# A distance-only bias in a fused attention and MLP kernel: forward and backward rows, put in place through a skewed DRAM scratch, in a new order

## The chip, the cores and the metric

The kernel runs on one core of one Trainium2 chip. A core has five engines that run side by side and meet at semaphores: PE (TensorE, matrix products), DVE (VectorE), ACT (ScalarE), POOL (GpSimd) and SP (SyncE, which here issues every DMA). The metric is device microseconds (us) of one execution, as the median of several. The profile is of one more execution of the same program.

## The reference

Three stages follow each other. `q`, `k` and `v` have the shape (2 batches, 8 heads, 576 positions, 64).

```python
scores = scale * np.matmul(q, k.transpose(0, 1, 3, 2))
psi_rel = np.log1p(np.abs(pos[:, None] - pos[None, :]))
psi_i = np.log1p(np.maximum(pos[:, None], 1.0))
x = (psi_rel / psi_i)[..., None]
h = np.maximum(x @ w1 + b1, 0.0)          # 32 hidden units
bias = h @ w2                             # one value per head
scores = scores + bias.transpose(2, 0, 1)[None]
attn = softmax(scores); out = attn @ v
# then, on 1152 tokens of 512 values:
h = x @ w_in; x = (h * clip(h + 3, 0, 6) / 6) @ w_out         # 512 -> 2048 -> 512
h = x @ w_in2; x = (rational function of h) @ w_out2          # 512 -> 2048 -> 512
```

The part that the change touches is `bias`: for each pair (i, j) of positions a 32-unit layer of one input, summed to 8 heads. For a fixed row i it depends on j through |i - j| alone. It is the same for both batches.

## The kernel before, in words

The first third of the kernel is attention, the rest the two MLPs. Attention goes by five chunks of query rows (`qc`): four of 128 rows and one of 64, which is taken for both batches at once. For a chunk and a pair of heads, `scores` puts q times k into PSUM (L473; L488 in the last chunk), `logits` on DVE adds the bias tile to it and takes the row maximum (L496), ACT takes the exponential (L662), PE transposes the result in pieces of three 128-column blocks (L680), ACT or DVE copies the pieces out (L688, L690), and `av` multiplies by v (L508). A table, `EV_ENG`, says which engine copies which piece, `OUT_ENG` the same for the copies behind `av` (L712, L714).

The bias of a chunk is a tile `biases[qc]` of 128 rows x (8 heads x 576 columns), from a pool of two buffers (`huge`). It is made by groups `G` of 16 rows, 36 groups in all. The 128 partitions hold 4 rows x 32 hidden units, so a group takes four *units* (`bias_unit`): `relu(psi + threshold)` over 576 columns, on DVE (L431) or ACT (L429) by the table `U_ENG`. `psi` is the table log1p(|distance|) of 1152 columns per partition, of which a unit reads a window of 576 that is shifted by the row; the last four groups use a second table. `bias_sums` (L438) sums the hidden units to heads: for each half of 288 columns four matmuls with 32 output partitions each into one PSUM bank, so two banks a group. `bias_scaled` scales each half into a row buffer `wk` on ACT (L447) or DVE (L449) by the table `SC_ENG`, and `bias_out` (L458) issues one DMA that puts the 16 x 8 rows of 576 values into `biases[qc]`, directly in SBUF. The rows of a group stand 8 apart in the chunk. `unit_logits` needs all groups of its chunk.

Units come in pairs in tiles of the pool `big` (11 buffers), row buffers from `wk` (5 buffers), PSUM banks of sums, transposes and `av` from one pool of 4 (`h`), and a pair's scores take the whole of the pool `ps2`.

Each of these steps is put in a list with `at(time, function, ...)`. The order in which the program is written, and so the order of instructions in each engine's queue, is a table of numbers, `ORDER`, over that list. Each engine works strictly through its own queue.

Of the kernel before, what the change touches and what calls it, by code (L numbers as in the profile page):

```python
# [31 lines left out]
W2 = 2 * S  # L32
PS0 = S - P
# [4 lines left out]
U_ENG = (1, 1, 0, 0, 0, 0, 0, 0, 1, 1, 0, 0, 0, 0, 0, 0, 1, 0, 0, 0, 0, 0, 1, 0, 0, 0, 1, 1, 0, 0, 1, 1, 0, 0, 0, 0, 0,  # L38
# [3 lines left out]
EV_ENG = (1, 1, 1, 1, 1, 1, 1, 0, 1, 1, 1, 0, 1, 0, 1, 1, 1, 0, 0, 0, 1, 1, 1, 1, 1, 1, 1, 0, 0, 1, 1, 1, 0, 0, 1, 0, 1,  # L42
# [3 lines left out]
OUT_ENG = (1, 1, 0, 0, 1, 1, 1, 0, 0, 1, 0, 0, 0, 0, 0, 1, 1, 0, 1, 0)  # L46
X_DVE = (0, 0, 0, 0, 0, 0, 0, 0, 0)
SC_ENG = (1, 1, 1, 1, 1, 1, 0, 0, 1, 0, 1, 1, 1, 1, 1, 1, 1, 1, 1, 1, 1, 1, 1, 1, 1, 1, 1, 1, 0, 1, 1, 1, 0, 0, 0, 0, 1,
    1, 1, 0, 1, 0, 0, 1, 0, 0, 1, 0, 1, 0, 0, 0, 0, 0, 0, 1, 0, 0, 0, 1, 0, 0, 0, 0, 0, 0, 0, 0, 0, 0, 0, 0)
PTX = (1,) * 20 + (0,) * 20  # L50
N_EARLY = 5
ORDER = (0, 26, 1, 2, 24, 25, 27, 16, 28, 29, 3, 4, 30, 34, 32, 22, 42, 35, 33, 43, 50, 48, 36, 40, 51, 49, 41, 320, 37,
# [177 lines left out]
def fused_kernel(ctx: ExitStack, tc, q, k, v, moe_w_in, moe_w_out, moe2_w_in, moe2_w_out,  # L230
# [116 lines left out]
    with tc.manual_schedule():  # L347
# [776 lines left out]
```

## Time and profile before

| | |
|---|---|
| median of 3 runs | 592.98 us (591.97 to 593.93) |
| profiled execution | 594.1 us, of which the span from the first to the last instruction is 592.3 us |
| attention | to about 190 us of the span |
| the two MLPs | from there to the end |
| PE busy over the span | 98% |
| DVE, ACT, POOL busy | 79%, 66%, 33% |

Times in the rows are microseconds from the start of the span. A matmul in fp32 is recorded as two, so `x32` of L438 is 16 matmuls, two groups. A busy share of PE counts the modelled end of a matmul, so the chain of work that ended last is the better witness of what bounds the end. The column PEclk is the granted clock of TensorE as a share of full speed.

### The profile page before, as it was taken

The page shows a single profiled execution, that of the slowest core. Times are in us where ns is not written, and L with a number is a line of the kernel's source. Part 1 is how long each engine was busy: PE and PEld are TensorE (multiplying, and loading weights), DVE is VectorE, ACT ScalarE, POOL GpSimd, SP SyncE. Part 2 cuts the span into 40 slices and gives each one's busy share as a digit, 9 for nine tenths or more (in the row PEclk, how much of TensorE's full clock was granted, in tenths as well). Part 3 has the DMA queues.
Part 4 walks back from the last instruction along what each step waited for, and adds up shares of the span by engine and source line. Part 5 has one row for each costly group of instructions (what it writes and reads, how often), then busy time and mean ns, then how long its engine had stood idle before and what let it go on. Part 6 is the DMA issues. An engine that isn't in the chain of part 4 may idle for free.

```text
span 592.3 us, 11318 instructions
## 1 busy us (share of the span) xinstructions
PE 578.5 (98%) x4291; PEld 509.7 (86%) x4291; DVE 467.8 (79%) x952; ACT 390.1 (66%) x806; POOL 197.1 (33%) x186
## 2 busy tenths in 40 slices
PE   5999999999999999999999999999999999999996
PEld 4458776777788999999999999998898989989985
DVE  7688987788786867685647489888899989999773
ACT  4897886787766636343232344688889878888861
POOL 1000010011005624232003220655576756766632
PEclk8899999999999999999999999999999999999999
DMA  7697423113515352443313122510111313200112
GB/s 220 141 296 168 116 65 87 54 42 99 166 59 178 107 176 77 143 145 140 107 35 91 53 79 100 178 41 32 45 64 39 97 44 107 72 0 1 37 54 71
DMA packets 32119, 56.63 MB, mean 96 GB/s; under 512 B 2488, under 2 KB 19128, under 8 KB 32064
## 3 DMA queue, kind: packets, MB, share of 16 engines
q1 hardware_dynamic: 32064, 55.91, 31.9%
q8 instruction: 33, 0.54, 0.4%
q14 instruction: 22, 0.18, 0.1%
HBM read 41.75 MB, written 2.36 MB: 74 GB/s over the span
## 4 chain that ended last, share of the span: by engine, by line
PE 94%; ACT 2%; DMA 2%; issue 1%; DVE 1%; SPq 0%; ACTq 0%; DVEq 0%
PE h L337 34%; PE y L1005 33%; PE h L508 7%; PE ps L473 7%; PE h L680 6%; PE h L438 5%; DMA kraw<-in_k_dram 2%; PE h L755 1%; ACT wk L447 1%; PE ps L488 1%; ACT big L429 1%; SPq L526 0%; DVE part L1035 0%; ACT big L662 0%; PE h L729 0%
## 5 line engine op out<-in xcount | busy, mean ns | idle before, releaser
L337 PE MATMUL h<-xt,huge 128*128 128x384 f32 x504 | 93.5, 335 | 0.0
L337 PEld LDWEIGHTS h<-xt,huge 128*128 128x128 f32 x504 | 88.2, 188 | 1.1
L855 POOL TENSOR_TENSOR huge<-wk,huge 128x512 fp32r<-128x512 f32 x28 | 36.1, 1296 | 94.8 <-ACT huge L846 69.1
L782 POOL TENSOR_TENSOR xt<-oT,xt 128x512 fp32r<-128x512 f32 x9 | 11.5, 1288 | 168.3 <-ACT xt L776 168.3
L496 DVE CUSTOM_DVE_ANT_0 big<-ps,huge 128x576 f32<-128x576 f32 (+1 forms) x72 | 52.6, 760 | 18.2 <-PE ps L473 16.1
L337 PE MATMUL h<-xt,big 128*128 128x384 f32 x360 | 66.6, 335 | 0.0
L899 ACT ACTIVATE e<-h,cons 128x384 f32<-128x384 f32 x43 | 25.0, 582 | 61.4 <-PE h L337 61.1
L951 POOL TENSOR_TENSOR e<-e,e 128x384 f32<-128x384 f32 x48 | 49.0, 1022 | 44.6 <-ACT e L939 38.8
L337 PEld LDWEIGHTS h<-xt,big 128*128 128x128 f32 x360 | 63.0, 188 | 0.5
L662 ACT ACTIVATE big<-big,mx 128x576 f32<-128x576 f32 (+1 forms) x72 | 56.1, 785 | 6.4 <-DVE mx L496 6.1
L924 POOL TENSOR_TENSOR gl<-e,gh 128x384 fp32r<-128x384 f32 x48 | 49.1, 1028 | 26.4 <-ACT gh L916 15.2
L337 PE MATMUL h<-xt,wp 128*128 128x384 f32 x288 | 53.9, 335 | 0.0
L337 PEld LDWEIGHTS h<-xt,wp 128*128 128x128 f32 x288 | 50.7, 188 | 1.1
L473 PE MATMUL ps<-kraw,rawq 64*128 64x288 f32 x256 | 41.4, 438 | 6.6 <-DMA kraw<-in_k_dram 5.7
L680 PEld LDWEIGHTS h<-csm,big 128*128 128x128 f32 x328 | 35.4, 142 | 8.9 <-issue 4.8
L438 PE MATMUL h<-big,wblk 128*32 128x288 f32 x576 | 41.8, 419 | 0.9 <-ACT wk L447 0.5
L431 DVE TENSOR_SCALAR big<-psw,thr 128x576 f32<-128x576 f32 x94 | 42.5, 511 | 0.0
L680 PE MATMUL h<-csm,big 128*128 128x128 f32 x328 | 41.5, 277 | 0.3 <-ACT xt L688 0.3
L916 ACT ACTIVATE gh<-h 128x384 fp32r<-128x384 f32 x43 | 21.1, 491 | 28.6 <-PE y L1005 19.8
L905 DVE SCALAR_TENSOR_TENSOR h<-e,h 128x384 f32<-128x384 f32 x43 | 24.0, 558 | 20.1 <-ACT e L899 20.0
L473 PEld LDWEIGHTS ps<-kraw,rawq 64*128 64x128 f32 x256 | 22.9, 190 | 19.1 <-issue 10.7
L855 POOL TENSOR_TENSOR big<-wk,big 128x512 fp32r<-128x512 f32 x21 | 27.1, 1296 | 35.8 <-ACT big L846 22.7
(125 smaller groups left out, 1330.4 us busy)
## 6 DMA issues: line engine op xcount, KB each, us to landing
big<-in_moe_w_in_dram SPq DMA_DIRECT2D x32, 512.0 KB, 3.7
big<-in_moe_w_out_dram SPq DMA_DIRECT2D x32, 512.0 KB, 3.5
huge<-wk SPq DMA_DIRECT2D x40, 288.0 KB, 4.2
kraw<-in_k_dram SPq DMA_DIRECT2D x4, 576.0 KB, 8.9
rawq<-in_q_dram SPq DMA_DIRECT2D x4, 512.0 KB, 7.6
vraw<-in_v_dram SPq DMA_DIRECT2D x8, 256.0 KB, 6.2
out_dram<-part SPq DMA_DIRECT2D x5, 256.0 KB, 2.0
out_dram<-psw SPq DMA_DIRECT2D x3, 256.0 KB, 2.7
```

The lines of the kernel that those rows point to most:

```text
L337: nc.tensor.matmul(ps, wx[:, c, :], xx[:, c, :], start=(i == c == 0), stop=(i == 2 and c == KC - 1))
L431: eng.tensor_scalar(dst, win, thr[:, g:g + 1], 0.0, op0=ALU.add, op1=ALU.max)
L438: nc.tensor.matmul(ps[32 * ct:32 * ct + 32, :HS], wblk.rearrange("p i h -> p (i h)"), units_of[G, ct][:, hf * HS:(hf + 1) * HS], start=Tru ...
L473: nc.tensor.matmul(ps[e][:, 512 - HS * (1 - c):512 + HS * c] if c else ps[e][:, 512 - HS:512], x[r, b, hp, :], kraw[r, hp, S * b + HS * c: ...
L496: nc.vector.tensor_tensor_reduce(ss, ps, biases[qc][:, h * S:h * S + n], op0=ALU.add, op1=ALU.min, scale=-0.125, scalar=3e38, accum_out=mx)
L508: nc.tensor.matmul(o[64 * e:64 * e + 64], vraw[:, m, 2 * hp + e, :], pt[e][:, coff + c, cols], start=(c == 0), stop=(c == 4), tile_positio ...
L662: nc.scalar.activation(ss, ss, AF.Exp, bias=mxs[u // 2][:, b, u % 2:u % 2 + 1], scale=-1.0, accum_out=sums[qc][:, b, h:h + 1])
L680: nc.tensor.transpose(ps[:, c - c0], pes[u][:, c * P:(c + 1) * P], ident)
L855: nc.gpsimd.tensor_tensor(lo, held.pop(("wt", it)).bitcast(F32), hi.bitcast(F32), op=ALU.subtract)
L924: eng.tensor_tensor(gl, src, gh.bitcast(F32), op=ALU.subtract)
L951: nc.gpsimd.tensor_tensor(vq, vq, ab, op=ALU.mult)
L1005: nc.tensor.matmul(ys[c][d][:, :TC if L == 0 else DM], lhs, rhs, start=(first and i == 0), stop=(last and i == 2))
```

## The change

A group is now 16 consecutive rows. Its units are computed for the distances 0, 1, ..., n - 1 alone, where n is the larger of `16 G + 16` and `576 - 16 G`: 576 for the first group, 304 in the middle, 576 for the last, and 15,840 columns over the 36 groups, where there were 20,736. All units read the same window of one table of 576 columns, and the second table with its load and its sign step is gone. `bias_sums` takes a whole bank of up to 512 columns at once and a second, short one where n is over 512: 44 banks, where there were 72. `bias_scaled` writes the sums into a row buffer of 591 values: forwards for j >= i, and backwards (a source with step -1) for j < i, in two pieces, or three where there are two banks: 80 pieces in all, where there were 72. `bias_out` now stores these rows into a scratch tile in DRAM with a row step of one element more than the pitch, which shifts each of the 16 rows by its own place. When all groups of a chunk are stored, `load_bias` loads the chunk's bias tile back, two heads to a DMA (four DMAs a chunk, eight for the last). `unit_logits` needs the load of its own two heads.

All tables are new. By them DVE makes 126 of the 144 units (ACT 18; before, 101 and 43), ACT makes 56 of the 80 scaled pieces (16,003 of their 21,276 columns; before, 37 of 72), ACT copies out 101 of the 112 transposed pieces (before 75) and all 20 results of `av` (before 9).

```diff
-W2 = 2 * S
-PS0 = S - P
+DPI = S + 32
+PSA = 512
...
-OUT_ENG = (1, 1, 0, 0, 1, 1, 1, 0, 0, 1, 0, 0, 0, 0, 0, 1, 1, 0, 1, 0)
+OUT_ENG = (1, 1, 1, 1, 1, 1, 1, 1, 1, 1, 1, 1, 1, 1, 1, 1, 1, 1, 1, 1)
...
-ORDER = (0, 26, 1, 2, 24, 25, 27, 16, 28, 29, 3, 4, 30, 34, 32, 22, 42, 35, 33, 43, 50, 48, 36, 40, 51, 49, 41, 320, 37,
+ORDER = (0, 25, 1, 21, 23, 2, 26, 16, 3, 22, 24, 27, 28, 5, 29, 4, 76, 30, 66, 32, 31, 77, 33, 41, 84, 34, 57, 42, 85,
...
-def row_base(G, ct):
-
-    qc, g = divmod(G, 8)
-    return P * qc + g + (32 if qc < 4 else 16) * ct
+def group_rows(G):
+
+    return 16 * G, 16 * G + 16
+
+
+def distances(G):
+
+    r0, r1 = group_rows(G)
+    return max(r1, S - r0)
+
+
+def bank_spans(G):
+
+    n = distances(G)
+    return [(0, n)] if n <= 512 else [(0, 512), (512, n)]
+
+
+def row_pieces(G):
+
+    r0, r1 = group_rows(G)
+    r = []
+    for i, (a, b) in enumerate(bank_spans(G)):
+        if min(b, S - r0) > a:
+            r.append((i, a, min(b, S - r0), False))
+        if min(b, r1) > max(a, 1):
+            r.append((i, max(a, 1), min(b, r1), True))
+    return r
...
+    psi = np.broadcast_to(np.log1p(np.arange(S, dtype=np.float32))[None, :], (P, S))
...
+    rows = np.arange(S).reshape(NG, 16)
...
         def bias_unit(G, ct, eng):
 
-            g, r = 4 * G + ct, row_base(G, ct)
+            g, n = 4 * G + ct, distances(G)
             if ct % 2 == 0:
-                two = BIG([P, 2, S], F32)
+                two = BIG([P, 2, n], F32)
                 units_of[G, ct], units_of[G, ct + 1] = two[:, 0], two[:, 1]
-            dst = units_of[G, ct]
-            win = psiw[:, S - r:2 * S - r] if G < 32 else psit[0][:, S - r:2 * S - r]
+            dst, win = units_of[G, ct], psiw[:, :n]
...
         def bias_sums(G):
 
-            for hf in range(2):
+            outs[G] = []
+            for a, b in bank_spans(G):
                 ps = BANK()
                 for ct in range(4):
-                    nc.tensor.matmul(ps[32 * ct:32 * ct + 32, :HS], wblk.rearrange("p i h -> p (i h)"),
-                                     units_of[G, ct][:, hf * HS:(hf + 1) * HS],
-                                     start=True, stop=True, tile_position=(0, 32 * ct))
-                outs[G, hf] = ps
-
-        def bias_scaled(G, hf, eng):
-            if hf == 0:
-                rows_of[G] = W([P, 2, HS], F32)
+                    nc.tensor.matmul(ps[32 * ct:32 * ct + 32, :b - a], wblk.rearrange("p i h -> p (i h)"),
+                                     units_of[G, ct][:, a:b], start=True, stop=True, tile_position=(0, 32 * ct))
+                outs[G].append((a, ps))
+
+        def bias_scaled(G, k, eng):
+
+            r0, r1 = group_rows(G)
+            i, a, b, back = row_pieces(G)[k]
+            if k == 0:
+                rows_of[G] = W([P, S + 15], F32)
+            a0, ps = outs[G][i]
+            src = ps[:, a - a0:b - a0]
+            if back:
+                src = bass.AP(tensor=src.tensor, offset=src.offset + b - a - 1, ap=[list(src.ap[0]), [-1, b - a]])
+                dst = rows_of[G][:, r1 - b:r1 - a]
+            else:
+                dst = rows_of[G][:, r1 - 1 + a:r1 - 1 + b]
             if eng is nc.scalar:
-                nc.scalar.activation(rows_of[G][:, hf], outs.pop((G, hf))[:, :HS], AF.Copy, scale=rps[:, G:G + 1])
+                nc.scalar.activation(dst, src, AF.Copy, scale=rps[:, G:G + 1])
             else:
-                nc.vector.tensor_scalar(rows_of[G][:, hf], outs.pop((G, hf))[:, :HS], rps[:, G:G + 1], None, op0=ALU.mult)
+                nc.vector.tensor_scalar(dst, src, rps[:, G:G + 1], None, op0=ALU.mult)
 
         def bias_out(G):
 
             qc, g = divmod(G, 8)
-            flat = rows_of.pop(G).rearrange("p a j -> p (a j)")
-            if qc not in biases:
+            if qc not in stored:
+                stored[qc] = T(dpool, [P if qc < 4 else 64, NH * DPI], F32, f"rows{qc}")
+            t = stored[qc]
+            dst = bass.AP(tensor=t.tensor, offset=t.offset + 16 * g * NH * DPI, ap=[[NH * DPI + 1, 16], [DPI, NH], [1, S + 15]])
+            nc.sync.dma_start(dst, rows_of.pop(G))
+
+        def bias_in(qc, hp):
+
+            if hp == 0:
                 new_bias(qc)
-            if qc < 4:
-                nc.sync.dma_start(biases[qc][g::8, :NH * S], flat)
-            else:
-                for rep in range(2):
-                    nc.sync.dma_start(biases[qc][64 * rep + g:64 * rep + 64:4, 64 * rep:64 * rep + NH * S], flat)
+            t, n = stored[qc], P if qc < 4 else 64
+            src = bass.AP(tensor=t.tensor, offset=t.offset + 15 + 2 * hp * DPI, ap=[[NH * DPI, n], [DPI, 2], [1, S]])
+            for rep in range(1 if qc < 4 else 2):
+                nc.sync.dma_start(biases[qc][n * rep:n * rep + n, 64 * rep + 2 * hp * S:64 * rep + 2 * (hp + 1) * S], src)
...
-        at(-9.9, load, "psiw1", psiw[:, PS0:], cpsi[:, PS0:W2])
-        at(-9.85, load, "psiw0", psiw[:, :PS0], cpsi[:, :PS0])
+        at(-9.9, load, "psiw0", psiw[:, :PSA], cpsi[:, :PSA])
+        at(-9.85, load, "psiw1", psiw[:, PSA:], cpsi[:, PSA:])
...
-        at(POS[4] - 14, load_psit)
...
+        def load_bias(qc, hp):
+            need(*(("out", G) for G in range(8 * qc, min(8 * qc + 8, NG))), *((("rows", qc, 0),) if hp else ()))
+            bias_in(qc, hp)
+            done.add(("rows", qc, hp))
...
-            for hf in range(2):
-                at(t + .65 + .05 * hf, group_scaled, G, hf, (nc.vector, nc.scalar)[SC_ENG[2 * G + hf]])
+            for i in range(len(row_pieces(G))):
+                at(t + .65 + .05 * i, group_scaled, G, i, (nc.vector, nc.scalar)[SC_ENG[3 * G + i]])
             at(t + .8, group_out, G)
+        for qc in range(5):
+            for hp in range(NPAIR):
+                at(POS[qc] - .1 + .02 * hp, load_bias, qc, hp)
...
             need(("scores", qc, h // 2, b))
-            need(*(("out", G) for G in range(8 * qc, min(8 * qc + 8, NG))))
+            need(("rows", qc, h // 2))
```

PE, the start of the program: `h` is a PSUM bank, `big` a pair of units, `ps` scores. Before:

```order
L566 MATMUL h_91<-ones_79 128x128 x13
L438 MATMUL h_137<-big_124,wblk_89 32x288 x2
L438 MATMUL h_137<-big_122,wblk_89 32x288 x2
L438 MATMUL h_142<-big_124,wblk_89 32x288 x2
L438 MATMUL h_142<-big_122,wblk_89 32x288 x2
L473 MATMUL ps_26_152<-kraw_83,rawq_114 128x288
```

The same place in the change:

```order
L600 MATMUL h_93<-ones_81 128x128 x13
L462 MATMUL h_143<-big_130,wblk_91 32x512 x2
L462 MATMUL h_143<-big_134,wblk_91 32x512 x2
L462 MATMUL h_148<-big_130,wblk_91 32x64 x2
L462 MATMUL h_148<-big_134,wblk_91 32x64 x2
L512 MATMUL ps_28_159<-kraw_85,rawq_117 128x288
```

One group stands ahead of the first scores in both. Behind these, 13 groups stand ahead of the second scores before, and 15 in the change; the first `av` has 17 groups ahead of it before, and 21 in the change.

SP, the DMA queue, from the last stores of chunk 0's bias on. Before, `huge` is the bias tile itself and the first row is the last but two of chunk 0:

```order
L458 DMA huge_178<-wk_273 16x8x576
L458 DMA huge_178<-wk_279 16x8x576
L458 DMA huge_178<-wk_311 16x8x576
L458 DMA huge_339<-wk_316 16x8x576
L387 DMA vraw_84<-in_v_dram 128x512
```

In the change, `rows_33` and `rows_69` are the scratch of chunks 0 and 1, and `huge_336` the bias tile of chunk 0:

```order
L491 DMA rows_33_175<-wk_275 16x8x591
L491 DMA rows_33_175<-wk_294 16x8x591
L412 DMA vraw_86<-in_v_dram 128x512
L491 DMA rows_69_318<-wk_302 16x8x591
L500 DMA huge_336<-rows_33_175 128x2x576
L491 DMA rows_69_318<-wk_321 16x8x591
L491 DMA rows_69_318<-wk_346 16x8x591
L491 DMA rows_69_318<-wk_352 16x8x591
L491 DMA rows_69_318<-wk_365 16x8x591
L500 DMA huge_336<-rows_33_175 128x2x576 x2
```

The first load of the bias tile waits for all stores of its chunk. The second and third stand behind four stores of the next chunk; the fourth follows only behind the other eight loads of v and the last load of k.

## Rows read from the trace of the kernel before

**Rows 1.** Page, busy time: engine, us, share of the span, instructions.
```profile
PE 578.5 (98%) x4291; PEld 509.7 (86%) x4291; DVE 467.8 (79%) x952; ACT 390.1 (66%) x806; POOL 197.1 (33%) x186
```
**Rows 2.** Page, the chain that ended last, by engine and by line.
```profile
PE 94%; ACT 2%; DMA 2%; issue 1%; DVE 1%; SPq 0%; ACTq 0%; DVEq 0%
PE h L337 34%; PE y L1005 33%; PE h L508 7%; PE ps L473 7%; PE h L680 6%; PE h L438 5%; DMA kraw<-in_k_dram 2%; PE h L755 1%; ACT wk L447 1%; PE ps L488 1%; ACT big L429 1%; SPq L526 0%; DVE part L1035 0%; ACT big L662 0%; PE h L729 0%
```
**Rows 3.** Windows, all engines: stretch, length, busy (instructions), clock, DMA share, GB/s.
```profile
core 0: us, PE busy (x) PEld busy (x) DVE busy (x) ACT busy (x) POOL busy (x), PEclk, DMA share, GB/s
0.00:33.00 33.00, 24.60 (x258) 13.31 (x258) 23.15 (x57) 20.64 (x39) 1.62 (x10) 0.90 0.71 189
33.00:48.07 15.07, 14.66 (x125) 8.81 (x125) 12.63 (x34) 13.76 (x36) 0.00 (x0) 1.00 1.06 292
48.07:70.00 21.93, 21.93 (x292) 17.26 (x294) 19.25 (x50) 17.95 (x42) 0.00 (x0) 1.00 0.54 137
70.00:105.00 35.00, 35.00 (x406) 24.75 (x399) 28.19 (x70) 27.26 (x63) 2.60 (x2) 1.00 0.33 83
105.00:140.00 35.00, 35.00 (x407) 26.74 (x406) 28.03 (x72) 27.80 (x65) 2.80 (x4) 1.00 0.21 55
140.00:175.00 35.00, 35.00 (x433) 26.86 (x428) 26.81 (x67) 25.41 (x62) 2.52 (x2) 1.00 0.38 108
```
**Rows 4.** Windows of L438 alone: PE and PEld busy (records), clock, DMA.
```profile
0.00:33.00 33.00, 17.55 (x224) 7.42 (x224) 0.90 0.71 189
33.00:48.07 15.07, 3.53 (x48) 1.25 (x48) 1.00 1.06 292
```
**Rows 5.** The chain in order of time: start, us, what.
```profile
3.55 10.04 DMA kraw<-in_k_dram
...
48.14 4.52 PE h L508 x80
...
59.45 2.08 PE h L438 x32
```
**Rows 6.** Timeline of DVE to 34 us: start, us, what, idle before it.
```profile
5.46 8.24 DVE L431 TENSOR_SCALAR big<-psw,thr 128x576 f32<-128x576 f32 x19
19.78 0.52 DVE L449 TENSOR_SCALAR wk<-h,csm 128x288 f32<-128x288 f32 x1 [6.09 <-PE h L438]
...
21.92 9.96 DVE L431 TENSOR_SCALAR big<-psw,thr 128x576 f32<-128x576 f32 x23
32.34 0.76 DVE L496 CUSTOM_DVE_ANT_0 big<-ps,huge 128x576 f32<-128x576 f32 x1 [0.46 <-PE h L438]
```
**Rows 7.** Groups by shape to 190 us: count, busy, mean ns, idle before.
```profile
L429 ACT ACTIVATE big<-psw,thr 128x576 f32<-128x576 f32 x34 | 25.1, 777 | 3.2 <-DVE psw L601 3.2
...
L688 ACT ACTIVATE xt<-h 128x384 f32<-128x384 f32 x42 | 18.1, 496 | 11.1 <-PE h L680 11.1
...
L447 ACT ACTIVATE wk<-h,csm 128x288 f32<-128x288 f32 x37 | 17.1, 514 | 3.7 <-PE h L438 2.8 <-DMA huge<-wk 0.9
...
L712 ACT ACTIVATE oT<-h 128x256 f32<-128x256 f32 x7 | 2.7, 385 | 1.6 <-PE h L508 1.5
...
L601 DVE TENSOR_SCALAR psw<-psw,tb 128x704 f32<-128x704 f32 x1 | 0.6, 577 | 0.0
...
L601 DVE TENSOR_SCALAR psw<-psw,tb 128x448 f32<-128x448 f32 x1 | 0.4, 443 | 0.0
```
**Rows 8.** DMA from 24 to 50 us: packets and issues, KB each, us to landing.
```profile
DMA packets 3246, 6.88 MB, mean 265 GB/s; under 512 B 376, under 2 KB 376, under 8 KB 3242
...
huge<-wk SPq DMA_DIRECT2D x11, 288.0 KB, 8.0
vraw<-in_v_dram SPq DMA_DIRECT2D x8, 256.0 KB, 6.2
```
**Rows 9.** Page, DMA issues of the whole run, us to landing.
```profile
big<-in_moe_w_in_dram SPq DMA_DIRECT2D x32, 512.0 KB, 3.7
...
huge<-wk SPq DMA_DIRECT2D x40, 288.0 KB, 4.2
...
out_dram<-part SPq DMA_DIRECT2D x5, 256.0 KB, 2.0
```

More of the change, by code (lines that the diff above doesn't have):

```diff
@@ L183 @@
 S_PSQ, S_RPS, S_MSK, S_ID, S_W, S_END = 0, 144, 180, 212, 340, 350
-def row_base(G, ct):
-    qc, g = divmod(G, 8)
-    return P * qc + g + (32 if qc < 4 else 16) * ct
+def group_rows(G):
[15 more added lines that the diff above has]
+    return r
 def _constants():
     p = np.arange(P)
-    u = np.arange(W2)[None, :]
-    psi = np.log1p(np.abs(np.concatenate([u - S - 8 * (p // HID)[:, None], u[:, :640] - S - 4 * (p // HID)[:, None]],
-                                         axis=1)).astype(np.float32))
+    psi = np.broadcast_to(np.log1p(np.arange(S, dtype=np.float32))[None, :], (P, S))
     psi_i = np.log1p(np.maximum(np.arange(S, dtype=np.float32), np.float32(1.0)))
-    rows = np.array([[row_base(G, ct) + (8 if G < 32 else 4) * il for ct in range(4) for il in range(4)] for G in range(NG)])
+    rows = np.arange(S).reshape(NG, 16)
     psq = psi_i[rows.reshape(144, 4)[:, p // HID].T]
@@ L203, in _constants @@
     sel = (np.arange(4 * P)[None, :] // HD == np.arange(NH)[:, None]).astype(np.float32)
-    return {"csel": sel, "cpsi": psi.astype(np.float32), "csmall": np.ascontiguousarray(small)}
+    return {"csel": sel, "cpsi": np.ascontiguousarray(psi), "csmall": np.ascontiguousarray(small)}
 def _rows(ap, parts, n):
@@ L349, in fused_kernel @@
         scores_ctx = ctx.enter_context(ExitStack())
+        dpool = ctx.enter_context(tc.tile_pool(name="dpool", bufs=1, space=DRAM))
         apool = actx.enter_context(tc.tile_pool(name="apool", bufs=1))
@@ L353, in fused_kernel @@
         csm = T(apool, [P, S_END], F32, "csm")
-        psiw = T(cpool, [P, W2], F32, "psw")
+        psiw = T(cpool, [P, S], F32, "psw")
         sel = T(apool, [NH, 4 * P], F32R, "sel")
@@ L395, in fused_kernel @@
         wblk = T(apool, [P, 4, NH], F32, "wblk")
-        psit = {}
         def bias_constants():
@@ L408, in bias_weights @@
                                     w2b.unsqueeze(1).to_broadcast([P, 4, NH]), op=ALU.mult)
-        biases, units_of, outs, rows_of = {}, {}, {}, {}
+        biases, units_of, outs, rows_of, stored = {}, {}, {}, {}, {}
         def new_bias(qc):
@@ L527, in load @@
             done.add(key)
-        def load_psit():
-            psit[0] = BIG([P, 640], F32)
-            load("psit", psit[0], cpsi[:, W2:])
         def load_x(fn, nm, m):
@@ L571, in group_unit @@
         def group_unit(G, ct, eng):
-            need(*((("psiw sign", 0),) + ((("psiw sign", 1),) if row_base(G, ct) > S - PS0 else ()) if G < 32 else ("psit sign",)))
+            need(("psiw sign", 0), *((("psiw sign", 1),) if distances(G) > PSA else ()))
             if ct % 2:
@@ L581, in group_sums, with group_scaled @@
             done.add(("sums", G))
-        def group_scaled(G, hf, eng):
-            need(("sums", G), *((("bias", G, 0),) if hf else ()))
-            bias_scaled(G, hf, eng)
-            done.add(("bias", G, hf))
+        def group_scaled(G, k, eng):
+            need(("sums", G), *((("bias", G, 0),) if k else ()))
+            bias_scaled(G, k, eng)
+            done.add(("bias", G, k))
         def group_out(G):
-            need(("bias", G, 0), ("bias", G, 1), *((("out", G // 8 * 8),) if G % 8 else ()))
+            need(*(("bias", G, k) for k in range(len(row_pieces(G)))), *((("out", G // 8 * 8),) if G % 8 else ()))
             bias_out(G)
+            del outs[G]
             done.add(("out", G))
+        def load_bias(qc, hp):
+            need(*(("out", G) for G in range(8 * qc, min(8 * qc + 8, NG))), *((("rows", qc, 0),) if hp else ()))
+            bias_in(qc, hp)
+            done.add(("rows", qc, hp))
         def bias_start():
@@ L598, in psiw_sign @@
         def psiw_sign(late):
-            need("thr", f"psiw{1 - late}")
-            part = psiw[:, :PS0] if late else psiw[:, PS0:]
+            need("thr", f"psiw{late}")
+            part = psiw[:, PSA:] if late else psiw[:, :PSA]
             nc.vector.tensor_scalar(part, part, sgn, None, op0=ALU.mult)
             done.add(("psiw sign", late))
-        def psit_sign():
-            need("thr", "psit")
-            nc.vector.tensor_scalar(psit[0], psit[0], sgn, None, op0=ALU.mult)
-            done.add("psit sign")
         def weights():
```

10 lines of the change are left out of this document (5 added, 5 removed), and 260 rows, old and new, of tables (EV_ENG, ORDER, U_ENG).

## The prediction, made before the changed kernel had run

> **What bounds the kernel now.** I read the page's busy shares first, then the chain that ended last, then windows over attention. The shares give PE 98% of the span [rows 1]; since a busy PE is not a PE at its peak, the chain is what settles it: 94% of it is PE, and the matmuls of the bias (L438) are 5% of the chain, some 30 us, although they compute nothing that ends up in an MLP [rows 2]. The windows show two parts of attention. To 48.07 us, where the first product with v begins [rows 5], PE is not the bound: it has 24.6 of 33 us at a granted clock of 0.90 [rows 3], it stands in its queue for the first k until 13.6 us [rows 5], DVE loses 6.09 us behind a copy that waits for PE, and the first logits come at 32.34 us [rows 6]. The DMA engines are full from then on: share 1.06 at 292 GB/s from 33 to 48 us [rows 3]. From 48.07 us PE is busy without a gap, 35.00 of every 35 us at clock 1.00, with DVE at 77 to 88% and ACT at 73 to 82% [rows 3]. So what is taken off PE behind 48 us comes off the end, if the others keep up; what is taken off ahead of it counts only as far as the first product with v comes earlier.
>
> **PE behind the first product with v.** Ahead of it L438 has 224 + 48 = 272 records [rows 4], 17 groups at 16 records, so 19 groups stand behind it. Two groups take 2.08 us there [rows 5], one 1.04 us: 19 x 1.04 = 19.8 us. In the change 21 groups stand ahead and 15 behind, with 352 to 576 distances each: 6,960 columns (352, 368, ... 576). By columns, 1.04 us / 576 = 1.8 ns each, they take 12.6 us. The gain is 7.2 us. No row shows a bank of 512 columns, nor the short second bank of 16 to 64 columns that four of these groups need. Its bounds: the short bank costs what its columns cost, 160 columns or 0.3 us in all four, or as much as a bank of 288, 0.52 us each, 2.1 us; then the gain is 5.4 us. At the other end, a tenth of a bank's price that does not depend on its columns would make 19 banks in place of 38 cheaper by another 0.3 us. I take 7.2, for the price follows columns wherever the banks are long, and these are nearly all.
>
> [...]
>
> **The opening, up to the first product with v.** Before the first logits, DVE had 44 units and 3 scaled halves: at 9.96 / 23 = 0.43 us a unit in a run [rows 6] these are 19 + 1.6 us from 5.46 us on, 26 us, and with the 6.09 us of idling 32.2, which is where the logits came. In the change 58 units of 455 columns on average stand ahead of the first logits. A unit gets shorter by 0.52 ns a column (577 less 443 ns for 256 columns [rows 7]), so it takes 0.43 - 121 x 0.00052 = 0.37 us, and all of them 21.4 us: 27 us without a stall. No scaled piece stands in DVE's queue there, so the 6.09 us as such go. What is late next is a buffer: the units have 11 buffers of two, and PE gives none back between the first group and the arrival of k, since the first scores stand in the same place of its queue. DVE fills its 11 by about 12 us (5.5 + 16 x 0.41) and goes on when the second group is summed at about 17 us: 5 us lost, 32 us for the first logits. The bounds are 27 and 33.
>
> Beside it runs the detour through DRAM. The units of chunk 0 are complete after 30 of DVE's units, about 23 us with that stall; one group's sums and scaling behind it make 25 us. Then the last store and the first load follow each other, where one transfer was: 4.2 us for a store if it goes as the bias rows did, 2.0 if it goes as the stores of the output, and 3.7 us for a load of similar size [rows 9]. That is 30.7 to 33 us, near the 32 of DVE. The load stands on SP behind the stores it waits for, and behind it stand four stores of chunk 1 and the second and third load; ACT, which has only 5 row buffers, waits for those stores.
>
> [...]
>
> What the transfers do to each other is the larger unknown. Up to the last chunk of v, SP's queue holds from the second group on 13 stores of 0.30 MB, 3 loads of 0.59 MB and 2.4 MB of v: 8.1 MB. Before, 10 stores, v, one q and one k made 6.4 MB. The 1.7 MB more take 6 us at the mean of 265 GB/s of this stretch [rows 8]; at worst, all of chunk 0's loads, 2.36 MB, come on top at that rate: 8.9 us. But before, the engines had room until about 24 us, and a store to DRAM, 2.0 us against 4.2 [rows 9], promises a better rate than the transfers inside SBUF that it replaces. So the first product with v comes between 44 us (the DVE bound, then the same 15.7 us from logits to product as before) and 57 us. I take 49.6, or 1.5 us later than before.
>
> **ACT.** By durations of [rows 7]: 43 units become 18 shorter ones, 33.4 less 11.7 = -21.7 us; scaling goes from 37 x 0.514 to 56 pieces, 28.7, or +9.7; 26 more copies of transposes at 0.496 (five of them narrower) +12.4; 11 more of the results +4.0. Together +4.4 us. DVE is relieved: the units cost no more (126 shorter against 101), while 11 scaled pieces, 26 transposed pieces and 11 results leave it. In PE's dense part ACT goes from 98.4 of 126.9 us, 78% [rows 3], to some 83%, and the wait that could come in place of the removed work is a PE transpose that finds no free bank because a copy waits in ACT's queue behind an exponential. Before, DVE took every third copy. Its bounds are 0 and the whole 4.4 us; I take 1.0, since at 80% PE had no gap.
>
> What has no price: the smaller psi table and the second table that goes come off a load and one DVE step that nothing waited for. The MLPs are unchanged, and their weights are loaded and split by DVE, ACT and POOL, which finish attention earlier too.
>
> **The sum**, against the profiled execution: 594.1 - 7.2 + 1.5 + 1.0 = 589.4 us. That execution is 1.1 us above the median shown, 592.98, so the same sum for a median is 588.3 us.
>
> **Rivals.** *The opening gets shorter.* If the buffers come back sooner, the first logits are nearer to 27 us and the product with v comes at 44: 594.1 - 7.2 - 4 + 1 - 1.1 = 582.8. For it: the stall behind the copy [rows 6] is gone. Against it: k comes no earlier, and the DMA queue is longer.
>
> *ACT becomes the bound of the dense part.* All 4.4 us stand on the path: 594.1 - 7.2 + 1.5 + 4.4 - 1.1 = 591.7. For it: ACT now has nine of ten copies that free PE's banks. Against it: 83% on average.
>
> *The detour through DRAM costs more than PE saves.* Its place is the stretch from 24 to 50 us, where the engines are full [rows 3, 8], and v stands behind three loads in one queue. With 2.36 MB at 265 GB/s, 8.9 us, it is 594.1 - 7.2 + 8.9 + 1 - 1.1 = 595.7. It decides from the point at which the first product with v begins later than 56 us. For it: every bias byte now moves twice, and each row of the scratch starts at another odd place, which no row here has. Against it: the mean of 265 GB/s is held down by the transfers inside SBUF, 8.0 us to landing against 6.2 for v [rows 8].
>
> **How the numbers follow.** This kernel's runs differ so that about 0.3%, 1.8 us, can be told from no change: 591.2 to 594.8 is no change. My forecast, 584 to 591 by its own bounds, has 0.52; the shorter opening 0.18; ACT as the bound 0.14; the costly detour 0.16. So faster 0.70, no change 0.14, slower 0.16. The range from 582 to 594.5 leaves out the costly detour and little below.
>
> **What the profile after would show.** L462 with about 32 us of busy time in place of 41.8, and groups behind the first product with v at 1.8 ns a column, say 0.92 us at 512; the first logits at 31 to 33 us; the first product with v at 48 to 52; PE without gaps from there, the waits on ACT's copies about 1 us in all. The forecast is wrong if PE waits for v or for a bias load for over 4 us, if waits of transposes or sums on ACT come to several us, if long banks cost more than their columns, or if the MLPs begin to wait for weights.

## The result, and the profile after

The changed kernel takes 584.59 us (median of four runs, 584.04 to 585.33) against 592.48 (591.85 to 593.93) for the kernel before on the same chip: a ratio of 0.9864 [0.984, 0.9889], 7.9 us less. The profiled execution took 585.12 us, with a span of 583.2 where it was 592.3.

The page of after, busy time, and the chain that ended last by engine, as [rows 1, 2]:

```profile
PE 572.6 (98%) x4067; PEld 503.5 (86%) x4067; DVE 450.7 (77%) x928; ACT 389.8 (67%) x837; POOL 198.2 (34%) x186
...
PE 93%; DMA 3%; DVE 2%; ACT 1%; SPq 0%; issue 0%; POOL 0%; DVEq 0%; ACTq 0%; POOLq 0%
```

PE still bounds the kernel, with 5.9 us less to do. Where the 9.1 us of span went shows when the span is cut at the first product with v (48.14 us before, 46.02 after) and at the end of attention. Windows of after, columns as in [rows 3]:

```profile
0.00:46.02 46.02, 40.92 (x312) 20.84 (x314) 38.05 (x110) 34.14 (x81) 1.61 (x10) 0.96 0.87 283
46.02:180.50 134.48, 134.48 (x1608) 104.17 (x1609) 92.49 (x237) 109.78 (x278) 12.54 (x12) 1.00 0.53 165
180.50:583.20 402.70, 397.25 (x2150) 378.50 (x2149) 320.13 (x582) 245.85 (x479) 184.01 (x165) 1.00 0.25 79
```

The opening is 2.1 us shorter; what follows the first product with v is 7.0 us shorter (592.3 - 48.14 = 544.2 before, 583.2 - 46.02 = 537.2). In the second window PE is busy in all of its 134.48 us, with ACT at 82%. Windows of L462, the sums of the bias, behind the first product with v: busy time (records):

```profile
46.02:190.00 143.98, 12.96 (x152) 3.95 (x152) 1.00 0.50 155
```

The same window of L438 before is

```profile
48.07:190.00 141.93, 20.72 (x304) 8.75 (x304) 1.00 0.35 96
```

so 7.8 us less there. How the opening runs now is read from the chain in order of time (start, us, what). It begins with `bcoef`, a load of 1 KB: a step of ACT that reads it (`babs`) stands ahead of the first scaled rows in ACT's queue.

```profile
3.88 5.99 DMA bcoef<-in_moe_b_dram
9.89 0.02 ACT babs L1092
...
12.90 6.42 PE h L462 x55
...
19.54 3.75 DMA rows<-wk
...
23.34 5.03 DMA huge<-rows
...
28.54 0.76 DVE big L535
...
30.33 1.23 PE ps L512 x6
...
46.02 4.52 PE h L547 x80
```

and from the timelines of DVE and of PE (start, us, what, idle before it):

```profile
5.32 21.33 DVE L454 TENSOR_SCALAR big<-psw,thr 128x496 f32<-128x496 f32 x58
28.54 0.76 DVE L535 CUSTOM_DVE_ANT_0 big<-ps,huge 128x576 f32<-128x576 f32 x1 [1.90 <-DMA huge<-rows]
```

```profile
9.00 1.24 PE L512 MATMUL ps<-kraw,rawq 64*128 64x288 f32 x8 [0.28 <-DMA kraw<-in_k_dram]
29.36 0.75 PE L512 MATMUL ps<-kraw,rawq 64*128 64x288 f32 x2 [1.61 <-DVE mx L535]
```

Three things differ from [rows 5, 6]. The first scores come at 9.00 us; before, PE waited for k, and they ran from 13.72 us, in a stretch with a granted clock of 0.50 (14 to 18 us), into which PE came after standing idle for k for 5.68 us. DVE makes its 58 units in one go, in 21.33 us, nearly the 21.4 that the prediction had worked out, without the 5 us of idle time that it put on top. And the first logits, at 28.54 us, wait for the detour: last store 3.75 us, first load 5.03 us, of which DVE waits out 1.90.

Why k is earlier is in the DMA rows to 16 us: KB each, us from issue to landing. Before, then after:

```profile
kraw<-in_k_dram SPq DMA_DIRECT2D x3, 576.0 KB, 10.0
rawq<-in_q_dram SPq DMA_DIRECT2D x1, 512.0 KB, 7.7
psw<-in_cpsi_dram SPq DMA_DIRECT2D x1, 352.0 KB, 3.2
...
psw<-in_cpsi_dram SPq DMA_DIRECT2D x1, 224.0 KB, 3.3
...
bcoef<-in_moe_b_dram SPq DMA_DIRECT2D x1, 1.0 KB, 7.0
```

```profile
kraw<-in_k_dram SPq DMA_DIRECT2D x3, 576.0 KB, 6.9
...
rawq<-in_q_dram SPq DMA_DIRECT2D x1, 512.0 KB, 4.5
psw<-in_cpsi_dram SPq DMA_DIRECT2D x1, 256.0 KB, 2.8
...
psw<-in_cpsi_dram SPq DMA_DIRECT2D x1, 32.0 KB, 2.7
...
bcoef<-in_moe_b_dram SPq DMA_DIRECT2D x1, 1.0 KB, 6.0
```

`bcoef` is a constant of the second MLP, 128 partitions of 8 bytes each. By the old order it was issued ahead of q and k, by the new one behind the first of both. It takes 7.0 and 6.0 us here, and 4.3 and 7.4 in the two runs below that move it. A second thing differs ahead of q and k: the psi table (`psw`), 576 KB in two loads before and 288 KB in the change.

### The profile page after: what moved, and what is told of

Its sections match the earlier page's. It is cut to its first block, busy times and chain, and to the rows that moved or that the text cites. A ratio compares the mean times of both kernels' runs of the same rounds, so it can differ in the third digit from the quotient of the medians.

```text
span 583.2 us, 10935 instructions
## 1 busy us (share of the span) xinstructions
PE 572.6 (98%) x4067; PEld 503.5 (86%) x4067; DVE 450.7 (77%) x928; ACT 389.8 (67%) x837; POOL 198.2 (34%) x186
## 4 chain that ended last, share of the span: by engine, by line
PE 93%; DMA 3%; DVE 2%; ACT 1%; SPq 0%; issue 0%; POOL 0%; DVEq 0%; ACTq 0%; POOLq 0%
PE h L361 34%; PE y L1042 32%; PE h L547 7%; PE h L717 7%; PE ps L512 6%; PE h L462 4%; DMA bcoef<-in_moe_b_dram 1%; PE h L792 1%; DMA huge<-rows 1%; DMA big<-in_moe_w_out_dram 1%; PE ps L527 1%; DMA rows<-wk 1%; DVE part L1072 0%; ACT wk L480 0%; DVE h L305 0%
## 5 line engine op out<-in xcount | busy, mean ns | idle before, releaser
L361 PE MATMUL h<-xt,huge 128*128 128x384 f32 x504 | 93.1, 335 | 0.9 <-DVE wk L307 0.9
L361 PEld LDWEIGHTS h<-xt,huge 128*128 128x128 f32 x504 | 88.0, 188 | 2.0 <-DVE wk L307 1.2
L361 PE MATMUL h<-xt,big 128*128 128x384 f32 x360 | 66.1, 334 | 0.0
L361 PEld LDWEIGHTS h<-xt,big 128*128 128x128 f32 x360 | 62.9, 188 | 0.5
L988 POOL TENSOR_TENSOR e<-e,e 128x384 f32<-128x384 f32 x48 | 49.0, 1020 | 37.8 <-ACT e L976 34.8
L361 PE MATMUL h<-xt,wp 128*128 128x384 f32 x288 | 52.8, 335 | 0.0
L361 PEld LDWEIGHTS h<-xt,wp 128*128 128x128 f32 x288 | 50.5, 188 | 0.6
L454 DVE TENSOR_SCALAR big<-psw,thr 128x336 f32<-128x336 f32 (+17 forms) x126 | 49.1, 456 | 0.0
L717 PEld LDWEIGHTS h<-csm,big 128*128 128x128 f32 x328 | 35.6, 142 | 8.1 <-issue 4.6
L717 PE MATMUL h<-csm,big 128*128 128x128 f32 x328 | 41.7, 279 | 0.0
L462 PE MATMUL h<-big,wblk 128*32 128x512 f32 (+17 forms) x352 | 35.8, 485 | 1.9 <-DVE big L454 1.2
L982 ACT ACTIVATE e<-h,acoef 128x384 f32<-128x384 f32 x48 | 32.0, 667 | 7.7 <-PE h L361 7.0
L1014 DVE SCALAR_TENSOR_TENSOR e<-e,acoef,h 128x384 f32<-128x384 f32 x48 | 29.1, 610 | 10.0 <-ACT h L1009 9.8
```

Source lines behind the costliest of these rows:

```text
L361: nc.tensor.matmul(ps, wx[:, c, :], xx[:, c, :], start=(i == c == 0), stop=(i == 2 and c == KC - 1))
L454: eng.tensor_scalar(dst, win, thr[:, g:g + 1], 0.0, op0=ALU.add, op1=ALU.max)
L462: nc.tensor.matmul(ps[32 * ct:32 * ct + 32, :b - a], wblk.rearrange("p i h -> p (i h)"), units_of[G, ct][:, a:b], start=True, stop=True, t ...
L717: nc.tensor.transpose(ps[:, c - c0], pes[u][:, c * P:(c + 1) * P], ident)
L988: nc.gpsimd.tensor_tensor(vq, vq, ab, op=ALU.mult)
```

## The experiments

Each kernel was timed beside the kernel before on the same chip, so ratios compare across all of them. One table for all: the median, the ratio with its 95% interval, and from the profiled execution the start of the first scores, first logits and first product with v (us), and the span less that start.

| kernel | us | ratio | scores | logits | product | rest |
|---|---|---|---|---|---|---|
| before (first profile) | 592.98 | 1 | 13.72 | 32.34 | 48.07 | 544.2 |
| after (first profile) | 584.59 | 0.9864 [0.984, 0.9889] | 9.00 | 28.54 | 45.95 | 537.2 |
| after_again | 584.25 | 0.9843 [0.9829, 0.9858] | 9.18 | 28.74 | 44.97 | 537.3 |
| after_third | 584.49 | 0.9851 [0.9839, 0.9864] | 8.95 | 28.52 | 44.94 | 537.3 |
| small_first | 586.04 | 0.9876 [0.9861, 0.9892] | 10.48 | 29.56 | 46.15 | 537.6 |
| before_k_first | 589.98 | 0.9948 [0.993, 0.9966] | 10.94 | 27.47 | 43.20 | 544.2 |
| all_columns | 588.20 | 0.9912 [0.9898, 0.9926] | 8.96 | 28.52 | 48.16 | 539.6 |
| before_copies | 587.72 | 0.9911 [0.9892, 0.9931] | 8.55 | 28.57 | 46.45 | 541.2 |
| before_new_copies | 595.41 | 1.0032 [1.0014, 1.005] | 13.17 | 31.53 | 48.31 | 545.5 |
| direct_0 | 592.72 | 0.9993 [0.9984, 1.0002] | 8.96 | 34.52 | 53.38 | 537.7 |
| direct_8 | 583.50 | 0.9842 [0.9821, 0.9863] | 8.63 | 26.68 | 44.42 | 537.0 |
| direct_7 | 583.50 | 0.9838 [0.9816, 0.9859] | 8.70 | 26.61 | 43.56 | 538.2 |
| late_small | 584.94 | 0.9859 [0.9847, 0.9872] | 8.46 | 27.77 | 45.17 | 537.7 |
| late_fill | 583.75 | 0.984 [0.982, 0.9861] | 8.61 | 27.63 | 44.42 | 539.3 |

The first profile of after holds a stretch at a lower clock in its opening (0.59 from 32 to 36 us); after_again and after_third don't, and their first product with v comes 1.0 us sooner. The last column is nearly a constant of its kernel, whatever the opening does (537.0 to 538.2 us for the changed dense part; late_fill's 539.3 stands below). So the two terms of the sum can be tried one at a time.

**The small load: after_again, small_first, before_k_first.** The changed kernel again, as the measure for the next two; then its load of `bcoef` (24 in the list of steps) moved ahead of the first q and k; and in the kernel before the same load (25 there) moved behind them.

```diff
 small_first
-ORDER = (0, 25, 1, 21, 23, 2, 26, 16, 3, 22, 24, 27, ...
+ORDER = (0, 25, 1, 21, 23, 24, 2, 26, 16, 3, 22, 27, ...
 before_k_first
-ORDER = (0, 26, 1, 2, 24, 25, 27, 16, 28, 29, 3, 4, ...
+ORDER = (0, 26, 1, 2, 24, 27, 16, 28, 29, 3, 25, 4, ...
```

> The changed kernel once more, as the measure for the runs beside it: 584.0 to 585.5 us, about 7.9 us below the kernel before.

> The changed kernel with one entry of the order moved: the 1 KB load of the coefficients b (bcoef) stands ahead of the first q and k, as it did before. Theory 1 (the opening is shorter because k comes 4.7 us earlier, past the small load that blocked it): k lands at about 13 us, the first scores begin there and not at 9.0, PE's clock falls to half, the first logits come at 31 to 33 us and the first product with v at 48 to 49; time 587 to 589. Rival (the opening is shorter because no scaled piece stands in DVE's queue ahead of the logits): first logits stay below 29.5 us, time within 0.7 us of the changed kernel.

> The kernel before with the same entry moved the other way: bcoef behind the first q and k. Theory 1: the first scores begin at about 9 to 10 us, DVE's 6 us of idling behind the copy shrink to under 2, the first logits come at 27 to 30 us in place of 32.3; 2 to 4 us faster than the kernel before, 588.5 to 590.5. Rival: the logits wait for bias transfers that are no sooner; within 0.7 us of the kernel before.

In the kernel before, that one moved load is worth 3.4 us (593.36 to 589.98). Between the profiled executions, which lie 4.9 us apart, the first product with v comes 4.9 us earlier and the rest stays at 544.2. Theory 1 held in the main: DVE's idle time of 6.09 us [rows 6] is gone, since the first scores come at 10.94 us in place of 13.72 (it had 9 to 10):

```profile
10.94 1.24 PE L350 MATMUL ps<-kraw,rawq 64*128 64x288 f32 x8 [1.06 <-DMA kraw<-in_k_dram]
```

In the changed kernel the old place costs 1.8 us, but not by the way that theory 1 had named, and its time of 587 to 589 was not reached. PE and DVE of small_first:

```profile
8.11 2.44 PE L337 MATMUL h<-big,wblk 128*32 128x512 f32 x16 [1.26 <-DVE big L329]
10.48 1.24 PE L387 MATMUL ps<-kraw,rawq 64*128 64x288 f32 x8
```

```profile
6.98 0.26 DVE L516 TENSOR_SCALAR psw<-psw,tb 128x64 f32<-128x64 f32 x1 [1.89 <-DMA psw<-in_cpsi_dram]
7.15 21.33 DVE L329 TENSOR_SCALAR big<-psw,thr 128x496 f32<-128x496 f32 x58
```

Here the first scores wait for the first units and not for k. The last 32 KB of the psi table, which now stand behind the load, take 4.02 us to land (2.7 in after), so that DVE begins its units at 7.15 us instead of 5.85 in after_again; then it makes all 58 without a stall.

When the first load of k lands (issue plus time to landing) parts two causes. In the kernel before it is at 13.6 us, and at 10.8 with the small load behind it; in the changed kernel it is at 8.9 with the small load behind (after), and at 10.48 at the latest with it ahead (small_first, whose first scores begin then without a wait for k). So the small load accounts for 2.8 us and for at most 1.6. The other 3.1 us or more, from 13.6 to 10.48, come with what else the change does ahead of k, above all the psi table of half the size. That table was not tried by itself, and a load of 16 KB (`csel`) changes its place too, so the table as the cause is not shown. The shorter opening belongs in part to a load that has nothing to do with the bias. Against a kernel before with the same repair, the change is worth 589.98 - 584.25 = 5.7 us.

**The columns: all_columns.** PE gets back the 4,896 columns that the shorter groups save, as further matmuls whose result the next ones overwrite.

```diff
+                more = S - distances(G) if a == 0 else 0
+                for ct in range(4 if more else 0):
+                    nc.tensor.matmul(ps[32 * ct:32 * ct + 32, :more], wblk.rearrange("p i h -> p (i h)"),
+                                     units_of[G, ct][:, :more], start=True, stop=True, tile_position=(0, 32 * ct))
```

> The changed kernel, but PE computes for each group as many columns as before (576): ahead of each group's sums four further matmuls fill the same bank with the missing columns, and the sums overwrite them; 4,896 columns more, on PE alone. Theory 1 (columns on PE behind the first product with v come off the end one for one, those ahead of it do not): 15 groups stand behind it with 1,680 columns more, 3.0 us, and the opening is 1 to 3 us later: 588 to 590.5. Rival A (every column counts): 8.8 us more, 593.4. Rival B (the gain is the order and the opening, PE has slack): below 585.5.

It takes 3.95 us more than after_again, within what theory 1 had forecast. The rest behind the first product with v is 539.6 us: with full columns but with four groups moved ahead, it is 4.6 us below before's 544.2, and the columns saved are the last 2.3. The split is of one profiled execution, 1.5 us above its median; its stretch at a lower clock lies in the opening (0.89 from 30 to 46 us). So most of what the dense part gains comes from where the groups stand in PE's queue, and less from their being shorter. That the kernel before could have moved four groups ahead too, with its longer units and without the new rows, was not tried.

**The copies: before_copies, before_new_copies.** The tables that share the copies out of PSUM between DVE and ACT, exchanged between the two kernels.

```diff
 before_copies (and the reverse in before_new_copies)
-OUT_ENG = (1, 1, 1, 1, 1, 1, 1, 1, 1, 1, 1, 1, 1, 1, 1, 1, 1, 1, 1, 1)
+OUT_ENG = (1, 1, 0, 0, 1, 1, 1, 0, 0, 1, 0, 0, 0, 0, 0, 1, 1, 0, 1, 0)
...
```

> The kernel after with the two tables that share copies out of PSUM between DVE and ACT taken from the kernel before; nothing else. Theory 1 (PE has no gap behind the first product with v, and waits for ACT or DVE are some 4 us in the whole span, so which of the two copies hardly matters): within 0.8 us of the kernel after. Rival (ACT and DVE are near their limit in the attention stage, and the new tables are part of the gain): 1.5 to 5 us more than the kernel after, with new waits of PE for ACT wk or DVE wk.

> The kernel before with the two tables that share copies out of PSUM between DVE and ACT taken from the kernel after (101 of 120 and 20 of 20 on ACT instead of 75 and 9); nothing else. Theory (the tables fit the bias work that stands beside them; on after the old ones cost 3.2 us): the kernel before gains nothing from the new ones, 592.5 to 598 us. Rival (the tables are a gain of their own, which would be there without the new bias): 589.5 to 591.5 us.

My theory of before_copies fell: the old tables cost the changed kernel 3.2 us, and the rest grows from 537.3 to 541.2 us (in a profiled execution that took 589.5, 1.8 above the median, so the growth of a median run may be nearer 3 us). PE's waits in before_copies (us in total, times, longest):

```profile
PE h L361 <- DVE wk L307: 1.4, 1, 1.4
...
PE h L717 <- DVE xt L727: 0.8, 2, 0.5
PE h L717 <- ACT big L699: 0.3, 1, 0.3
```

The wait of L361, in the MLPs, is 0.8 us in after_third; the two of the transposes (L717) aren't there, and of theirs 0.8 us lie behind the first product with v. The rest of the 3.9 us isn't seen as waits. Of the records from 44 us on, 295 of L717 take 38.6 us against 36.4 for 292 in after_third, and the 216 of the scores 34.8 against 34.1; whether these hold waiting, the trace doesn't say. With the old tables ACT is busy for 72% of the time from 48 to 188 us and DVE for 77%, in after_third 80 and 68%. On the kernel before, the new tables cost 2.1 us. So they are no gain of their own: they go with the work on DVE that the change brings, and without them about half of what the dense part gains is lost.

**The detour: direct_0, direct_8, direct_7.** The first chunk's bias goes straight from the row buffers into its tile, without the skew. So its values land in the wrong places, and these three show a time only.

```diff
         def bias_out(G):
             qc, g = divmod(G, 8)
+            if qc == 0:
+                if qc not in biases:
+                    new_bias(qc)
+                nc.sync.dma_start(biases[qc][16 * g:16 * g + 16, :NH * S], rows_of.pop(G)[:, 15:S + 15])
+                return
...
 direct_8: biases[qc][g::8, :NH * S]
 direct_7: biases[qc][g:112:7, :NH * S] if g < 7 else biases[qc][112:, :NH * S]
```

> The kernel after, but the bias of the first query chunk goes from its row buffer to its tile in one transfer inside SBUF (columns 15 to 591 of each row), without the store to DRAM and the skewed load. The skew is left out for that chunk, so its bias is put in the wrong places. Theory 1 (the detour ends last ahead of the first logits: store 3.75 us, then load 5.03 us, and DVE waits 1.9 us for the load): first logits at 26.4 to 27.3 instead of 28.5 to 28.7, the first product with v earlier by 1 to 2 us, the time 1 to 2 us less than that of the kernel after in the same call. Rival A (the detour is free even here, since DVE's and ACT's own work in the opening would end no earlier): first logits within 0.3 us, the time within 0.5 us. Rival B (the store and the load are slow together with everything on the queue, and what stands behind them on it gains too): more than 2.5 us less.

> The kernel direct_0 (after, the first chunk's bias taken straight from its row buffers to the tile inside SBUF, skew left out), but the 16 partitions that a group's transfer writes are every eighth one, as in the kernel before, and not 16 adjacent ones. The skew and the order of the queries are left out for that chunk. [...] Rival (what made direct_0 slow is the source, which starts 60 bytes into its row, or the transfer inside SBUF as such beside the loads of v): 100 to 140 GB/s again, first logits after 33, 591.5 to 593.5 us.

> [...] The skew and the order of the queries are left out for the first chunk. [...]

direct_0 fell the other way: 8.2 us slower than the changed kernel, with the first logits at 34.52 us. The DMA rows from 14 to 26 us of direct_0, direct_8 and direct_7 (the first line: the rate in 40 slices of 0.3 us):

```profile
GB/s 78 169 138 123 177 123 115 92 100 123 123 123 123 138 115 115 123 108 84 100 131 192 123 115 69 92 135 92 115 146 146 131 108 92 115 123 123 108 84 100
DMA packets 679, 1.42 MB, mean 118 GB/s; under 512 B 72, under 2 KB 72, under 8 KB 677
...
huge<-wk SPq DMA_DIRECT2D x6, 288.0 KB, 11.2
```

```profile
DMA packets 1283, 2.64 MB, mean 220 GB/s; under 512 B 135, under 2 KB 135, under 8 KB 1281
...
huge<-wk SPq DMA_DIRECT2D x6, 288.0 KB, 5.9
```

```profile
GB/s 55 146 169 138 361 315 253 307 231 192 207 238 284 307 327 261 338 315 277 254 246 253 184 146 123 100 115 131 123 176 311 232 207 229 261 356 369 391 408 394
DMA packets 1411, 2.92 MB, mean 243 GB/s; under 512 B 145, under 2 KB 145, under 8 KB 1409
...
huge<-wk SPq DMA_DIRECT2D x6, 288.0 KB, 5.3
```

In the mean of these 12 us the DMA moves 118 GB/s where the bytes go into 16 adjacent partitions, and 220 where the same bytes from the same source go into every eighth one, while the packets took 101 and 98% of the 16 DMA engines' time. In direct_7 they go at 192 to 361 where every seventh is written, and at 100 to 184 where its last group writes 16 adjacent ones. From 15.2 to 20.6 us, where little else is under way, the means of the three are 122, 231 and 276 GB/s. The forecast for direct_8 was 200 to 215 GB/s, as in the kernel before, which writes every eighth partition too, and 584.5 to 589 us: the rate came out above, the time below, and its rival, 100 to 140 GB/s again, fell. What ties the rate to the partitions written, no run shows; if only adjacency counted, 276 should lie within 10% of 231. On the time direct_7 has no edge over direct_8 (583.50 us both), since DVE's units end last by then (logits at 26.61 and 26.68 us, DVE's idle time gone).

So writing the new groups of 16 consecutive rows straight to adjacent partitions would have cost 8.2 us for one chunk alone. The DRAM scratch does without that transfer: in the same stretch of after_third, at 241 GB/s in the mean, its stores took 3.9 us, and its first load, which writes all 128 partitions, 4.8. Compared with direct_8, it delays the first logits by 1.8 us; the times, 583.50 and 584.49, are too near for their intervals to part them.

**A better opening: after_third, late_small, late_fill.** The changed kernel once more, as the measure for late_small, before_copies and direct_0. Then `bcoef` and a second small load, `acoef` of 2 KB, moved back to about 40 us, with them ACT's step on `bcoef` (the third of the "small loads" of the text below is this step), and the one load of v that stood ahead of the first bias load put behind it. Then that and six spare matmuls in PE's wait at 28.6 us.

```diff
 late_small
-ORDER = (0, 25, 1, 21, 23, 2, 26, 16, 3, 22, 24, 27, 28, ...
+ORDER = (0, 25, 1, 21, 2, 26, 16, 3, 22, 27, 28, ...
 late_fill, in addition
+        filled = []
...
         def pair_scores(qc, hp, b):
...
+            filled.append(0)
+            if len(filled) == 2:
+                fill = BANK()[:, :P]
+                for _ in range(6):
+                    nc.tensor.matmul(fill, ones, ones, start=True, stop=True)
```

> The kernel after, unchanged, as the measure for the other three of this call: 583.6 to 585.4 us, 0.984 to 0.989 of the kernel before. Theory 1 (its own spread of 1 us comes from whether PE's wait of 1.6 us ahead of the second scores is followed by a stretch at a lower granted clock): a span of 582.2 to 582.5 with a granted clock of 1.00 from 20 to 46 us, or 583.2 to 583.5 with a dip to about 0.5 just behind that wait. Rival (the spread has another cause): a span and a dip that don't go together.

> The kernel after with the three small loads of 8-byte pieces moved further back in the opening (the first two behind the first load of v, the third, which ACT prepares, behind the attention) and the first load of v's second chunk behind the first bias load. Theory 1 (in the kernel after these small loads still hold up later ones: q takes 4.5 us and k 5.5, and ACT waits 2.2 us for one of them): first scores at 8.0 to 9.0, first logits 27.3 to 28.5, 0.5 to 1.5 us less than the kernel after. Rival (what bounds the first logits is DVE's 58 units of bias and the detour, neither of which starts earlier): within 0.4 us.

> The kernel late_small with six matmuls of ones into a spare bank ahead of the second pair's scores, to keep PE busy in its wait of 1 us at 28.6 us. Theory (that wait is followed by a stretch at half clock, 28 to 36 us, which costs 0.7 to 1 us): granted clock 1.00 from 20 to 46 us, first product with v 0.5 to 1 us earlier than late_small's 45.2, 583.8 to 584.5 us in each run. Rival (the clock falls here whatever PE does in the wait, or the added work costs what the clock gives): within 0.3 us of late_small's 584.94, or more.

late_small brings the first logits 0.75 us forward and no time (0.9859 against 0.9851): its rival was right. Windows of late_small, then of late_fill (the third number from the end is the granted clock):

```profile
28.00:32.00 4.00, 3.19 (x14) 2.11 (x14) 4.00 (x14) 3.42 (x9) 0.00 (x0) 0.83 1.03 332
32.00:36.00 4.00, 4.00 (x31) 1.83 (x30) 3.02 (x8) 3.13 (x8) 0.00 (x0) 0.74 1.00 377
```

```profile
28.00:32.00 4.00, 4.00 (x34) 2.76 (x32) 4.00 (x14) 3.57 (x9) 0.00 (x0) 1.00 1.05 320
32.00:36.00 4.00, 3.83 (x34) 2.44 (x30) 4.00 (x13) 4.00 (x11) 0.00 (x0) 1.00 1.01 367
```

Behind the wait of 1.02 us ahead of its second scores PE gets 0.83 and 0.74 of its clock as means of these windows; in after, behind its wait of 1.61 us, windows of 1 us show 0.50 from 32 to 35 us. With the wait filled it keeps 1.00, and the first product with v comes 0.75 us earlier. The wait alone doesn't decide, though: in after_third the same wait is 1.31 us long, and the clock stays at 1.00:

```profile
29.34 0.75 PE L512 MATMUL ps<-kraw,rawq 64*128 64x288 f32 x2 [1.31 <-DVE mx L535]
```

```profile
28.00:32.00 4.00, 2.47 (x16) 1.50 (x14) 3.48 (x12) 2.79 (x8) 0.00 (x0) 1.00 1.01 321
32.00:36.00 4.00, 3.95 (x38) 2.22 (x36) 3.88 (x11) 4.00 (x12) 0.00 (x0) 1.00 0.99 348
```

So that the filling kept the clock up is not shown by one execution. The median of late_fill is 583.75 us, 1.2 below late_small's, the lowest of the kernels that compute the whole reference. But one of its five runs took 585.59 (the profiled one, in which the rest is 539.3 us, with 1.8 us of waits of PE for ACT's copies and for v), and its interval overlaps those of the changed kernel: not shown to be better. The clock explains the changed kernel's own spread of 1 us only in part: of the first four executions two had a mean clock of 1.00 and spans of 582.1 us, two 0.996 and 0.997 and 583.2 and 583.4, but in after_third spans of 582.7 and 582.8 us had 1.00 and one of 582.2 had 0.998. The remainder stays open.

## Why the prediction was right, and where it was not

**What bounds the kernel** held: behind the first product with v the end moves with PE's work (7.0 us less of span, 7.8 less of the sums of the bias).

**PE behind the first product with v, 7.2 us:** 7.0 measured, and 12.96 us for the 15 groups against 12.6. The price by columns held in sum: 12.96 us for 6,960 columns are 1.86 ns each, and 20.72 us for the 10,944 columns before 1.89. For a single record it doesn't: in the dense part those of 512 to 352 columns last 600 to 459 ns, which falls by less than the columns do. The short second banks cost more than their columns: the rows by shape there put 0.2 to 0.3 us on each, 1.0 us for the four (partly beside other records), against 0.3 by columns and a bound of 2.1. A record of 16 columns still lasts less than one of 64 (181 and 219 ns). all_columns shows how the term is made up: 4.6 us for the groups moved ahead, 2.3 for columns.

**The opening, +1.5 us:** -2.1 measured, and -3.1 in after_again and after_third; this step failed. The failing sentence is that the stall is "5 us lost", for PE gives no buffer back "between the first group and the arrival of k": k was taken to arrive as late as before, 13.6 us. The first scores came at 9.0, the 11 buffers never ran out, and 58 units took 21.33 us, the forecast without a stall being 21.4. What stands ahead of k was part of the change, and I had put it at nothing: the smaller psi table was to "come off a load and one DVE step that nothing waited for", but k stands behind that load in the queue (in after issued at 3.41 us, the table's two parts at 1.20 and 2.47), and I had not gone through the order for the one tiny load that moved past q and k. before_k_first shows that an earlier k ends DVE's stall, which is worth 3.4 us in the kernel before. small_first shows that the tiny load is not the whole cause: with it back in its old place k is still there by 10.48 us and DVE doesn't stall. Between the psi table and the rest of the new queue the cause stays open. The rival "the opening gets shorter" named the right mechanism, buffers that come back sooner, and, as evidence against itself, the same mistake ("k comes no earlier").

**The detour** was put at 25 us plus a store of 2.0 to 4.2 and a load of 3.7. It measured 3.75 and 5.03 us and begins at 19.54, so it is, and not DVE, what the first logits wait for. The traffic of 24 to 50 us did not grow into the costly rival: the rows there read

```profile
DMA packets 3855, 8.37 MB, mean 322 GB/s; under 512 B 378, under 2 KB 378, under 8 KB 3852
...
rows<-wk SPq DMA_DIRECT2D x9, 295.5 KB, 6.5
```

8.37 MB at 322 GB/s in place of 6.88 at 265 [rows 8]. The argument against that rival, that the old mean was held down by the transfers inside SBUF, fits direct_0 and direct_8, in which such transfers took 11.2 and 5.9 us to land by the partitions that they write.

**ACT, +1.0 us:** nothing in the dense part, where PE has no wait at all; 0.7 us of waits of L462 for ACT in the opening. That holds for these tables only: with the old ones this part of the profiled execution was 3.9 us longer.

**The sum** with the measured terms: 592.3 - 7.0 - 2.1 = 583.2 us of span. The forecast of 588.3 missed the median by 3.7 us. Between the profiled executions the terms missed by 4.4: 3.6 in the opening and 1.0 for ACT, less the 0.2 by which the dense part gained too little. That the time still lies inside 584 to 591, at its edge, is luck: it is nearer to the rival's 582.8 than to the forecast, and the rival's opening is the one that came.

## What to carry to other kernels

Cut the trace at the point from which the bounding engine has no gap: here what lies behind it and what lies ahead could be forecast and tried apart, and four groups moved across that point gave 4.6 us, twice what shorter groups behind it gave. Of a new order, read everything that stands ahead of the load that the opening waits for: here one load of 1 KB moved its landing by 2.8 us in the kernel before, and what else had changed ahead of k by 3.1 or more. Before writing rows straight from SBUF to SBUF, look at which partitions they land in: the same bytes took 11.2 us or 5.9.

## What the runs showed of the hardware

A load of 1 KB in pieces of 8 bytes took 4.3 to 7.4 us to land in the opening (6.0 in after, where the 512 KB of q ahead of it took 4.5), and its place in the queue changed a kernel's time by 1.8 and 3.4 us. Transfers inside SBUF went at 122 GB/s into sixteen adjacent partitions, at 231 into every eighth and at 276 into every seventh, from 15.2 to 20.6 us, where little else was under way. A wait of PE of 1.02 us was followed by granted clocks of 0.83 and 0.74 in two windows of 4 us, and by none below 1.00 when six matmuls of ones filled it; in another kernel a wait of 1.31 us at the same place was followed by 1.00, so what decides is open.
